# One fused attention and feed-forward kernel, its instruction order replaced by another searched one

## The chip, the cores and the metric

The kernel runs on one core of one Trainium2 chip. The metric is the device time of one execution in microseconds (us), lower is better.

## What is computed

The reference is a linear attention with a complex decay, and a gated feed-forward layer on its output. Batch 4, 8 heads, 768 positions, 48 columns to a head, so 384 columns together; 1024 hidden columns.

```python
mag = np.sqrt(a_re * a_re + a_im * a_im)
scale = np.minimum(mag, 0.999) / (mag + 1e-06)
for t in range(S):                       # per batch and head, S_re and S_im 48 x 48
    new_re = ar * S_re - ai * S_im
    new_im = ar * S_im + ai * S_re
    S_re, S_im = (new_re + kv, new_im)   # kv = outer(k_t, v_t)
    y[:, :, t] = np.einsum('bhd,bhde->bhe', q[:, :, t], S_re)
# x = y with heads side by side; x_prev = x one position earlier
xk = mu_k * x + (1.0 - mu_k) * x_prev
xr = mu_r * x + (1.0 - mu_r) * x_prev
k = np.maximum(xk @ w_k, 0.0)
v = k * k @ w_v
r = 1.0 / (1.0 + np.exp(-(xr @ w_r)))
return r * v
```

## The kernel before, in words

The 4 x 768 positions are cut into 8 units of 384: units 0 and 1 are the two halves of batch 0, and so on. Each unit goes through three phases.

- **gate** (phase `g`): loads the decay, k and q of the unit (`in_gat`, L720, tile `g`) and v (`in_vt`, L727), turns the decay into running logarithms (scans, L797) and phases (scans, L821) on ScalarE (ACT) and VectorE (DVE), and multiplies k and q with them (L811, and L864 as the last step). ACT needs four function tables for it and for the sigmoid; a change of table is the operation L321.
- **attend** (phase `a`): copies parts of `g` to the stacked tile `q` by DMA (L895), transposes keys on TensorE (PE) (L1021, L957), makes the sums of keys and values (L1060 in unit 0, L990 later), adds them up into states on DVE (L1073, L1000), makes scores (L1107, L1102), masks them on DVE (L1123, tile `pt`), and multiplies states and scores with queries and values (L1148). The result is copied from PSUM (L1183) to the tile `xt`; that of head pair 3 goes to `ys` and from there by six small DMAs (L1199) into `xt`. Unit 0 does this pair by pair, the others by two teams of pairs.
- **mix** (phase `m`): the shifted mixes of x (unit 0: L443 on ACT and L447 on DVE; others: L431, L458, a rounded first half L467 or L469 and the rest L472), the first product (L498 in unit 0, L502 later, where each operand is split in two halves and three products are made), relu on ACT (L545), square (L550 on DVE or L552 on ACT), the halves of h (L557 on DVE or ACT, L561 on DVE), the second product (L591), the sigmoid gate (`zr`) and the output (L618, stored by L623).

The weights come in ten pieces (phase `f`, L658, tile `raw`), are put together (phase `w`: L672 and L678, tile `wx`) and are split for units 1 to 7 (phase `s`: L697, L700). 75 fillers of two matmuls each on zeros (phase `x`, L1237) fill PE while unit 0's gate runs.

Nothing schedules at run time or by rules. Each phase records its operations in a `Plan`, and the table `ORDER` gives each operation a place, by phase and unit; `run` sorts by the places and emits, so that the five engines and the DMA queue of SyncE (SP) get their instructions in this order and work them off in it. A data or buffer dependence becomes a wait of the instruction. Two more tables belong to the order: `ON_DVE` names the operations, out of those that both engines can do, that DVE does (the rest is ACT's), and `HOMES` says which buffer of a pool each use takes.

```python
order = [next(places[phase]) if places else i for i, (_, _, phase) in enumerate(self.ops)]
self.queue = sorted(range(len(order)), key=order.__getitem__)
```

Table loads are not in the order: one is emitted ahead of an operation whose function the loaded table lacks.

Of the kernel before, what the change touches and what calls it, by code (L numbers as in the profile page):

```python
# [48 lines left out]
    ("g", 0): (0, 2, 1, 3, 4, 8, 10, 70, 5, 6, 22, 30, 36, 37, 43, 44, 59, 61, 63, 47, 75, 80, 84, 89, 88, 60, 78,  # L49
        79, 85, 92, 87, 81, 82, 83, 101, 103, 108, 90, 91, 111, 110, 137, 93, 94, 100, 102, 143, 109, 121, 114, 117,  # L50
        140, 99, 105, 134, 106, 125, 126, 97, 98, 133, 107, 130, 135, 95, 96, 119, 104, 115, 116, 131, 139, 141, 144,
        142, 136, 145, 161, 138, 156, 157, 172,),
    ("g", 1): (7, 15, 25, 235, 237, 234, 309, 320, 310, 162, 163, 164, 174, 194, 201, 211, 213, 222, 230, 227, 236,
        344, 267, 265, 278, 292, 277, 276, 314, 322, 325, 348, 326, 335, 336, 341, 345, 342, 361, 343, 364, 349, 360,),
    ("g", 2): (287, 295, 288, 472, 474, 112, 354, 357, 367, 384, 393, 400, 413, 414, 415, 425, 427, 424, 444, 445,
        446, 448, 455, 458, 467, 464, 531, 469, 477, 485, 486, 496, 490, 509,),
    ("g", 3): (451, 449, 450, 470, 656, 721, 557, 565, 568, 576, 593, 594, 613, 618, 621, 634, 625, 628, 718, 641,
        645, 650, 622, 644, 640, 633, 659, 669, 671, 688, 693, 700, 698, 714,),
    ("g", 4): (624, 681, 680, 880, 853, 951, 737, 756, 758, 772, 773, 779, 796, 797, 805, 808, 811, 816, 851, 817,
        821, 843, 815, 826, 832, 844, 863, 845, 847, 850, 860, 868, 861, 877,),  # L60
    ("g", 5): (820, 813, 812, 684, 1100, 1032, 893, 894, 916, 922, 935, 957, 960, 966, 968, 974, 970, 969, 1018,
        994, 985, 996, 1003, 1016, 1006, 1004, 1019, 1022, 1023, 1031, 1041, 1046, 1045, 1048,),
    ("g", 6): (999, 998, 1000, 1248, 1238, 1085, 1049, 1053, 1058, 1079, 1097, 1098, 1152, 1162, 1161, 1165, 1179,
        1163, 1181, 1193, 1194, 1195, 1103, 1189, 1167, 1182, 1205, 1202, 1203, 1218, 1219, 1228, 1229, 1233,),
    ("g", 7): (1220, 1188, 1186, 1300, 1487, 1399, 1268, 1272, 1289, 1308, 1329, 1330, 1334, 1338, 1343, 1344, 1356,
        1345, 1614, 1364, 1368, 1406, 1372, 1402, 1407, 1403, 1455, 1409, 1413, 1414, 1422, 1429, 1425, 1432,),
    ("f", 0): (12,),
    ("f", 1): (9,),
    ("f", 2): (50,),
    ("f", 3): (19,),  # L70
    ("f", 4): (67,),
    ("f", 5): (40,),
    ("f", 6): (56,),
    ("f", 7): (32,),
    ("f", 8): (311,),
    ("f", 9): (323,),
    ("w", 0): (71, 182,),
    ("w", 1): (54, 188,),
    ("w", 2): (199, 259,),
    ("w", 3): (200, 260,),  # L80
    ("w", 4): (263, 328,),
    ("w", 5): (299, 338,),
    ("w", 6): (329, 379,),
    ("w", 7): (380, 383,),
    ("w", 8): (421, 431,),
    ("w", 9): (456, 460,),
    ("a", 0): (122, 179, 149, 191, 146, 165, 166, 167, 168, 170, 184, 196, 203, 205, 208, 216, 221, 246, 154, 160,
        158, 239, 243, 242, 229, 212, 219, 197, 169, 173, 171, 186, 187, 190, 193, 204, 209, 210, 215, 217, 226, 177,
        181, 178, 261, 279, 266, 273, 238, 248, 240, 189, 206, 202, 218, 224, 220, 284, 290, 291, 293, 297, 301, 358,
        151, 176, 192, 185, 195, 175, 256, 257, 255, 225, 241, 244, 245, 247, 251, 254, 275, 249, 253, 250, 258, 264,  # L90
        269, 270, 271, 281, 280, 285, 283, 286, 300, 294, 306, 307, 316, 315, 308, 272, 282, 317, 377,),
    ("a", 1): (363, 402, 386, 397, 419, 430, 436, 365, 368, 417, 389, 401, 388, 371, 405, 426, 428, 390, 362, 382,
        391, 394, 392, 369, 370, 381, 395, 396, 399, 406, 411, 412, 374, 378, 376, 398, 409, 404, 418, 423, 429, 432,
        441, 433, 420, 440, 422, 442, 443, 452, 453, 457, 479, 447, 462, 459, 463, 475, 471, 481, 476, 487, 488, 480,
        492, 483, 505, 489, 493, 506,),
    ("a", 2): (543, 537, 519, 567, 559, 517, 513, 518, 595, 504, 578, 574, 515, 544, 514, 590, 554, 510, 586, 570,
        545, 558, 546, 541, 549, 551, 534, 535, 539, 555, 556, 587, 560, 566, 561, 577, 580, 579, 599, 601, 602, 538,
        552, 553, 536, 547, 542, 609, 610, 611, 630, 629, 637, 631, 623, 632, 635, 648, 653, 651, 674, 654, 661, 655,
        663, 658, 676, 678, 662, 664, 679, 803,),
    ("a", 3): (790, 744, 723, 750, 708, 763, 754, 774, 780, 703, 704, 716, 782, 709, 727, 751, 715, 733, 752, 722,  # L100
        728, 748, 735, 747, 757, 762, 734, 740, 749, 764, 765, 766, 741, 767, 742, 745, 770, 771, 776, 777, 783, 781,
        787, 786, 785, 788, 793, 804, 806, 825, 822, 835, 829, 807, 823, 824, 830, 838, 841, 839, 831, 856, 846, 870,
        849, 848, 872, 857, 871, 873,),
    ("a", 4): (874, 881, 911, 914, 952, 948, 937, 879, 913, 941, 926, 864, 865, 890, 950, 927, 882, 910, 891, 895,
        938, 939, 963, 896, 904, 899, 900, 919, 920, 928, 929, 930, 905, 924, 931, 942, 971, 947, 978, 981, 982, 945,
        946, 972, 949, 967, 979, 980, 983, 995, 984, 1002, 1005, 1012, 992, 1011, 1010, 1020, 1026, 1027, 1025, 1021,
        1034, 1050, 1029, 1073, 1067, 1033, 1051, 1074, 1068, 1089,),
    ("a", 5): (1059, 1109, 1125, 1054, 1099, 1128, 1083, 1087, 1093, 1047, 1092, 1084, 1094, 1124, 1066, 1055, 1127,
        1060, 1101, 1121, 1069, 1090, 1080, 1081, 1108, 1130, 1075, 1077, 1076, 1131, 1144, 1145, 1122, 1135, 1132,
        1117, 1139, 1138, 1140, 1148, 1151, 1153, 1168, 1154, 1146, 1170, 1171, 1173, 1174, 1175, 1176, 1177, 1183,  # L110
        1184, 1187, 1185, 1192, 1204, 1196, 1212, 1214, 1236, 1216, 1207, 1208, 1290, 1215, 1237, 1209, 1291,),
    ("a", 6): (1234, 1232, 1262, 1282, 1309, 1269, 1284, 1315, 1270, 1301, 1252, 1253, 1235, 1292, 1274, 1283, 1251,
        1302, 1275, 1239, 1303, 1320, 1335, 1266, 1271, 1267, 1258, 1259, 1294, 1295, 1306, 1307, 1263, 1264, 1265,
        1313, 1322, 1314, 1350, 1352, 1353, 1310, 1346, 1312, 1316, 1321, 1318, 1357, 1358, 1359, 1369, 1375, 1385,
        1386, 1354, 1379, 1378, 1380, 1387, 1382, 1383, 1384, 1392, 1393, 1390, 1388, 1389, 1397, 1394, 1391, 1398,
        1533,),
    ("a", 7): (1427, 1459, 1444, 1433, 1437, 1491, 1443, 1451, 1426, 1485, 1481, 1501, 1445, 1464, 1435, 1486, 1434,
        1458, 1497, 1460, 1488, 1510, 1517, 1449, 1470, 1466, 1456, 1477, 1480, 1482, 1483, 1493, 1494, 1496, 1504,
        1492, 1513, 1505, 1518, 1523, 1524, 1498, 1520, 1521, 1452, 1484, 1467, 1522, 1525, 1537, 1526, 1540, 1543,
        1519, 1529, 1530, 1534, 1542, 1535, 1554, 1539, 1571, 1544, 1546, 1545, 1555, 1556, 1572, 1547, 1557,),  # L120
    ("m", 0): (302, 304, 303, 372, 305, 319, 333, 407, 318, 332, 337, 434, 330, 331, 334, 339, 340, 312, 321, 346,
        347, 359, 366, 324, 327, 350, 356, 373, 385, 313, 351, 352, 375, 410, 403, 353, 355, 387, 408, 416, 435, 491,
        499, 501, 502, 503, 454, 437, 438, 439, 465, 466, 520, 497, 498, 500, 512, 524, 581, 582, 516, 530, 511, 522,
        507, 508, 588, 589, 605, 608, 583, 585,),
    ("m", 1): (494, 523, 532, 533, 521, 527, 528, 540, 584, 603, 604, 548, 562, 563, 550, 572, 575, 686, 564, 569,
        571, 710, 711, 705, 729, 701, 712, 591, 592, 598, 600, 612, 596, 597, 606, 607, 617, 636, 616, 638, 639, 660,
        668, 646, 614, 619, 649, 652, 670, 685, 657, 672, 673, 692, 697, 689, 677, 683, 702, 707, 713, 717, 665, 675,
# [29 lines left out]
        1686, 1688, 1687, 1697, 1693, 1689, 1699, 1700, 1694, 1696, 1692, 1695,),  # L157
    ("s", 0): (461, 468,),
    ("s", 1): (473, 478,),
    ("s", 2): (482, 484,),  # L160
    ("s", 3): (495, 525,),
    ("s", 4): (526, 529,),
    ("s", 5): (573, 615,),
# [1234 lines left out]
```

## Time and profile before

| what | value |
|---|---|
| median of 3 runs (from, to) | 399.31 us (397.34, 399.97) |
| the profiled execution, by the same clock as the runs | 399.91 us |
| its span in the trace | 398.1 us |
| PE busy | 381.8 us (96%), 5855 matmul passes |
| DVE busy | 336.0 us (84%) |
| ACT busy | 291.0 us (73%) |
| granted clock of PE over the span | 0.997 |

The page gives the busy time of each engine over the whole span; a list by stretches shows how that differs along the way, and the rows below take it from there. A wait in the trace is idle time of an engine ahead of an instruction, with what ended it; "issue" stands where the profile shows nothing that it waited for. Matmul ends are modelled, so short waits of PE can lie inside its busy time.

### The profile page before, as it was taken

How to read it: one execution, taken by the hardware profiler on the slowest of the kernel's cores; microseconds unless marked ns; L12 is line 12 of the kernel's file. 1: busy time of each engine (PE TensorE's matmuls, PEld its weight loads, DVE VectorE, ACT ScalarE, POOL GpSimd, SP SyncE). 2: the span in 40 equal slices, each digit the busy share in tenths (PEclk: the TensorE clock that was granted, in tenths of full speed). 3: DMA queues.
4: the chain of work that ended last, by engine and by line, in shares of the span. 5: the costliest groups of instructions: out<-in, count | busy, mean ns of one | idle time of the engine just before them, and what ended most of it. 6: DMA issues, size and time to landing. Idle time of an engine off the chain costs nothing. (4 is left out here: it accounts for less than half of the span.)

```text
span 398.1 us, 13663 instructions
## 1 busy us (share of the span) xinstructions
PE 381.8 (96%) x5855; PEld 349.4 (88%) x5855; DVE 336.0 (84%) x542; ACT 291.0 (73%) x556; POOL 23.8 (6%) x36
## 2 busy tenths in 40 slices
PE   6988889999999999899999999999999999999995
PEld 6977756675899999799989999999999999999994
DVE  6999999999999999899999978988999754555532
ACT  7997889989999996999668875778676721262420
POOL 5203100000000330000000100000000000000000
PEclk9999999999999999999999999999999999999998
DMA  8995466472431544714262331464011420100101
GB/s 272 419 400 103 155 251 219 101 273 62 121 101 63 181 114 130 261 40 122 66 250 86 96 97 56 155 207 107 4 67 31 109 66 4 66 9 2 61 2 64
DMA packets 23138, 49.70 MB, mean 125 GB/s; under 512 B 4864, under 2 KB 16640, under 8 KB 23072
## 3 DMA queue, kind: packets, MB, share of 16 engines
q1 hardware_dynamic: 23072, 48.78, 37.9%
q8 instruction: 47, 0.77, 0.8%
q14 instruction: 19, 0.16, 0.1%
HBM read 31.06 MB, written 4.72 MB: 90 GB/s over the span
## 5 line engine op out<-in xcount | busy, mean ns | idle before, releaser
L502 PE MATMUL bank<-x,w 128*128 128x384 f32 x693 | 127.6, 337 | 0.9 <-ACT xt L1183 0.9
L502 PEld LDWEIGHTS bank<-x,w 128*128 128x128 f32 x693 | 120.1, 188 | 2.2 <-ACT xt L1183 1.0
L591 PE MATMUL o<-hx,w 128*128 128x384 f32 x504 | 94.9, 337 | 0.0
L591 PEld LDWEIGHTS o<-hx,w 128*128 128x128 f32 x504 | 87.3, 188 | 0.2
L545 ACT ACTIVATE r<-bank 128x384 f32<-128x384 f32 x64 | 30.8, 488 | 41.6 <-PE bank L502 34.9
L864 DVE TENSOR_TENSOR g<-g,r 128x768 f32<-128x768 f32 (+1 forms) x24 | 41.7, 1754 | 0.5
L321 ACT ACT_TABLE_LOAD x29 | 37.2, 1283 | 1.3 <-PEq L1387 0.8
L561 DVE TENSOR_TENSOR hx<-h,hx 128x384 fp32r<-128x384 f32 x56 | 30.8, 554 | 5.6 <-ACT hx L557 4.9
L333 ACT ACTIVATE sq<-m 128x1152 f32<-128x1152 f32 (+1 forms) x30 | 28.3, 968 | 7.2 <-DVE m L797 5.0
L1237 PE MATMUL room<-idle 128*128 128x384 f32 (+4 forms) x150 | 29.8, 354 | 3.2 <-POOL idle L392 3.2
L1237 PEld LDWEIGHTS room<-idle 128*128 128x128 f32 x150 | 26.8, 198 | 4.2 <-POOL idle L392 3.2
L472 DVE TENSOR_TENSOR x<-xm,x 128x384 fp32r<-128x384 f32 x42 | 23.1, 552 | 6.3 <-ACT x L469 6.1
L552 ACT ACTIVATE h<-r 128x384 f32<-128x384 f32 x47 | 24.7, 526 | 4.8 <-DMA out_t<-y 2.7
L1148 PEld LDWEIGHTS bank<-q,state 112*48 112x48 f32 x704 | 21.4, 123 | 6.7 <-issue 4.2
L1148 PE MATMUL bank<-q,state 112*48 112x64 f32 x704 | 24.1, 221 | 3.3 <-DVE state L1073 1.4
L1107 PE MATMUL bank<-g 48*64 48x64 f32 x1200 | 25.0, 223 | 2.2 <-DVE g L864 1.1
L1107 PEld LDWEIGHTS bank<-g 48*64 48x64 f32 x1200 | 22.4, 133 | 4.7 <-issue 2.2
L458 DVE SCALAR_TENSOR_TENSOR xm<-dx,mu_sb,xt 128x384 f32<-128x384 f32 x42 | 25.4, 614 | 0.7
L1000 DVE TENSOR_TENSOR state<-bank,state 112x384 f32<-112x384 f32 x35 | 19.4, 554 | 7.5 <-ACT kt L971 3.3
L1209 POOL COPY last<-xt 128x3 f32<-128x3 f32 x4 | 9.9, 2468 | 247.8 <-DMA xt<-ys 164.1
L469 ACT ACTIVATE x<-xm 128x384 fp32r<-128x384 f32 x34 | 17.8, 524 | 6.8 <-DVE xm L458 5.8
L557 ACT CAST hx<-h 128x384 fp32r<-128x384 f32 x34 | 17.5, 514 | 7.1 <-PE o L591 4.2
(97 smaller groups left out, 581.1 us busy)
## 6 DMA issues: line engine op xcount, KB each, us to landing
g<-in_gat SPq DMA_DIRECT2D x18, 768.0 KB, 6.0
raw<-in_w_all SPq DMA_DIRECT2D x9, 767.8 KB, 13.7
v<-in_vt SPq DMA_DIRECT2D x24, 192.0 KB, 3.8
out_t<-y SPq DMA_DIRECT2D x24, 192.0 KB, 2.0
g<-in_gat SPq DMA_DIRECT2D x11, 384.0 KB, 4.6
q<-g SPq DMA_DIRECT2D x84, 48.0 KB, 2.3
q<-g SPq DMA_DIRECT2D x28, 144.0 KB, 2.9
q<-g SPq DMA_DIRECT2D x40, 72.0 KB, 2.2
```

The lines of the kernel that those rows point to most:

```text
L321: nc.scalar.add_instruction(mybir.InstLoadActFuncSet(name=nc.get_next_instruction_name(), act_func_set_id=n, engine=mybir.EngineType.Activ ...
L333: nc.scalar.activation(out=out, in_=in_, func=func, **kw)
L458: nc.vector.scalar_tensor_tensor(out=xm[which, ct], in0=d[ct], scalar=mu_sb[:, which, ct:ct + 1], in1=X[u][:, ct, 0:U], op0=ALU.mult, op1= ...
L502: nc.tensor.matmul(z, lhsT=wt[s[0]][:, part, s[1]], rhs=r[which][:, ct], start=n == 0, stop=n == 3 * NT - 1)
L545: nc.scalar.activation(out=t["r", j], in_=t["f", j], func=AF.Relu, scale=1.0 / W_SCALE)
L552: nc.scalar.activation(out=t["h", j], in_=t["r", j], func=AF.Square)
L561: plain[0].tensor_tensor(out=t["lo", j], in0=t["h", j], in1=t["hi", j].bitcast(F32), op=ALU.subtract)
L591: nc.tensor.matmul(tiles["o", mt][:, cols], lhsT=w, rhs=r[:, cols], start=j == 0 and n == 0, stop=j == NJ - 1 and n == len(parts) - 1 and ...
L864: nc.vector.tensor_tensor(out=g[:, d, 2 * i:2 * i + 2], in0=g[:, d, 2:4], in1=t["r"][:, 1 - i, d].unsqueeze(2).to_broadcast([P, k, 2, U]), ...
L1107: nc.tensor.matmul(y, lhsT=g[:, 2 * i, q], rhs=g[:, 2 * i + 1, q], start=i == 0, stop=i == 1)
L1148: nc.tensor.matmul(t["y", team][s][rows, h // 2 - team[0], c], lhsT=lhsT[:, cols], rhs=rhs, start=(s, h % 2) not in begun, stop=stop)
L1237: nc.tensor.matmul(room[0][:, :n], lhsT=idle[:, :P], rhs=idle[:, :n], start=True, stop=True)
```

## The change

The tables `ORDER`, `ON_DVE` and `HOMES` are replaced; every operation, its operands and its sizes stay. The new tables come from a search over three replays, two of them with late transfers, late refills and longer elementwise work. One line more in `ON_DVE` moves line numbers behind it up by one (L1183 is L1184 after).

```diff
@@ ORDER: all lists; three of them, cut @@
-    ("g", 0): (0, 2, 1, 3, 4, 8, 10, 70, 5, 6, 22, 30, 36, 37, 43, 44, 59, 61, 63, 47, 75, 80, 84, 89, 88, 60, 78,
...
@@ ON_DVE @@
     "abs": (
-        (0, 0), (0, 1), (1, 0), (3, 0), (4, 0), (5, 0), (6, 0), (7, 0),
+        (0, 2), (1, 0), (3, 0), (4, 0), (5, 0), (6, 0),
     ),
     "hi": (
-        (1, 4), (1, 7), (2, 0), (2, 2), (2, 3), (2, 4), (2, 6), (3, 2), (3, 3), (3, 4), (3, 6), (4, 3), (5, 4),
-        (5, 6), (5, 7), (6, 2), (6, 6), (6, 7), (7, 0), (7, 4), (7, 6), (7, 7),
+        (1, 3), (1, 5), (1, 6), (2, 2), (2, 7), (3, 2), (3, 4), (3, 5), (3, 6), (4, 1), (4, 2), (4, 3), (4, 4),
+        (4, 6), (5, 0), (5, 1), (5, 2), (5, 3), (5, 4), (5, 6), (6, 4), (7, 0), (7, 1), (7, 2), (7, 3), (7, 4),
+        (7, 6), (7, 7),
     ),
     "n": (
-        (0, 1), (4, 0), (5, 0),
+        (4, 0), (6, 0),
     ),
     "sq": (
-        (0, 0), (0, 1), (3, 4), (3, 5), (3, 6), (4, 2), (4, 3), (4, 5), (5, 1), (5, 6), (6, 1), (6, 2), (6, 4),
-        (6, 6), (7, 1), (7, 4), (7, 5),
+        (0, 2), (3, 4), (3, 5), (3, 7), (4, 2), (4, 5), (4, 6), (5, 0), (5, 6), (6, 4), (6, 5), (7, 3), (7, 4),
+        (7, 7),
     ),
     "xr": (
-        (1, 2), (2, 0), (2, 1), (3, 0), (5, 1), (6, 1), (7, 0), (7, 1),
+        (1, 2), (2, 1), (3, 0), (3, 1), (4, 0), (5, 2), (6, 0), (6, 1), (7, 0), (7, 1),
     ),
     "y": (
-        (0, 1, 1, 0), (0, 3, 0, 0), (1, 2, 0, 0), (1, 2, 1, 0), (4, 3, 1, 0), (5, 0, 1, 0), (5, 3, 0, 0), (5, 3,
-        1, 0), (5, 2, 0, 0), (5, 2, 1, 0), (6, 0, 0, 0), (6, 0, 1, 0), (7, 0, 1, 0), (7, 3, 0, 0),
+        (1, 2, 1, 0), (3, 2, 1, 0), (4, 3, 1, 0), (4, 2, 1, 0), (5, 2, 1, 0), (6, 3, 0, 0), (7, 0, 0, 0), (7, 3,
+        1, 0), (7, 2, 1, 0),
     ),
@@ HOMES: all but "g"; one of them @@
-    "kt": "010011110011101100010001",
+    "kt": "010000010010010100010101",
```

In `ON_DVE` a key's first number is the unit. "sq" is the square, "hi" the rounded first half of h, "xr" that of a mix, "y" the copy out of PSUM, "n" and "abs" two steps of the phase.

Three places show what that does to the engines. The first is ACT at the end of unit 0's attention, where the results of pairs 1 and 3 are copied out of PSUM (`xt`, `ys`) and the first mix begins (`x`, L443); before, and after it the same place now:

```order
L333 ACTIVATE sq<-m 128x3x384 x2
L1183 COPY ys<-bank 112x3x64
L321 ACT_TABLE_LOAD
L333 ACTIVATE ph<-ph 128x1152
L1183 COPY xt<-bank 112x3x64
L1075 COPY state_109<-bank 112x96
L672 CAST hx<-raw 128x768
L443 ACTIVATE x,stat<-xt,mu_118 128x384
```

```order
L334 ACTIVATE sq<-m 128x3x384 x2
L1184 COPY xt<-bank 112x3x64 x2
L1184 COPY ys<-bank 112x3x64 x2
L322 ACT_TABLE_LOAD
L334 ACTIVATE ph<-ph 128x1152
L1076 COPY state_109<-bank 112x96
L673 CAST hx<-raw 128x768
L444 ACTIVATE x,stat<-xt,mu_118 128x384 x2
```

Both copies of `ys` stand on ACT now, ahead of the table load, where one stood there and one on DVE. The second place is DVE at the same time, from two weight conversions (`wx`) to the first step of the mix (`x`, L447); before, and now:

```order
L678 SCALAR_TENSOR_TENSOR wx<-raw,hx 128x768 x2
L1183 COPY ys<-bank 112x3x64
L1183 COPY xt<-bank 112x3x64
L1073 TENSOR_TENSOR state_108<-bank,state_113 112x96
L811 TENSOR_TENSOR g<-g,sq 128x768 x2
L1073 TENSOR_TENSOR state_110<-bank,state_109 112x96
L811 TENSOR_TENSOR g<-g,sq 128x768
L1073 TENSOR_TENSOR state_111<-bank,state_110 112x96
L1123 TENSOR_TENSOR pt<-bank,mask 128x192
L1073 TENSOR_TENSOR state_112<-bank,state_111 112x96
L1123 TENSOR_TENSOR pt<-bank,mask 128x192
```

```order
L679 SCALAR_TENSOR_TENSOR wx<-raw,hx 128x768 x2
L812 TENSOR_TENSOR g<-g,sq 128x768 x3
L1074 TENSOR_TENSOR state_110<-bank,state_109 112x96
L1124 TENSOR_TENSOR pt<-bank,mask 128x192
L1074 TENSOR_TENSOR state_111<-bank,state_110 112x96
L1124 TENSOR_TENSOR pt<-bank,mask 128x192
L1074 TENSOR_TENSOR state_112<-bank,state_111 112x96
L1074 TENSOR_TENSOR state_113<-bank,state_112 112x96
L1074 TENSOR_TENSOR state_108<-bank,state_113 112x96
L448 SCALAR_TENSOR_TENSOR x<-xt,mu_sb,x 128x384
```

The two copies out of PSUM, `ys` and `xt`, are gone from DVE, and three products (L811) stand together. The third place is SP's queue at the end of unit 0's weight loads, with the first transfers from `g` to the stacked queries (`q01`, `q23`); before, and now:

```order
L658 DMA raw_267<-in_w_all 128x3071
L727 DMA v_273<-in_vt 128x384
L1244 DMA mu_sb_105<-in_mu 128x6
L727 DMA v_324<-in_vt 128x384
L895 DMA q01_114<-g_149 48x384 x2
```

```order
L659 DMA raw_300<-in_w_all 128x3071
L896 DMA q01_114<-g_151 48x384
L728 DMA v_365<-in_vt 128x384
L1245 DMA mu_sb_105<-in_mu 128x6
L896 DMA q01_114<-g_151 48x384
L728 DMA v_438<-in_vt 128x384
L728 DMA v_442<-in_vt 128x384
```

Before, two `v` loads of unit 0 stood among the first seven transfers (not shown) and two more here (one of them of unit 1), ahead of the first `q01`; now the first three `v` loads stand behind it. Further on in the same queue the last `q23` transfer of unit 0 stood between the second and third of the six `xt<-ys` transfers, and stands now ahead of all six.

## Rows read from the trace of the kernel before

**Rows 1.** Stretches: length, busy us (instructions) of PE, PEld, DVE, ACT, POOL; clock, DMA.

```profile
25.00:52.30 27.30, 22.27 (x615) 18.67 (x614) 26.17 (x51) 22.72 (x43) 5.00 (x3) 1.00 0.56 164
...
62.00:165.00 103.00, 101.86 (x1867) 85.28 (x1867) 100.31 (x151) 94.22 (x166) 7.48 (x1) 1.00 0.44 136
...
165.00:265.00 100.00, 98.25 (x1561) 94.45 (x1555) 92.77 (x138) 77.96 (x145) 1.05 (x1) 1.00 0.39 122
...
265.00:393.40 128.40, 127.97 (x1679) 124.44 (x1679) 86.21 (x156) 65.39 (x144) 0.50 (x1) 1.00 0.17 48
```

**Rows 2.** Waits of PE over the span: us in total, times, longest.

```profile
PE bank L1148 <- DVE state L1073: 1.4, 1, 1.4
...
PE bank L1148 <- DMA q<-g: 1.2, 1, 1.2
...
PE bank L1148 <- issue: 1.1, 2, 0.7
...
PE bank L1107 <- issue: 1.1, 2, 0.9
...
PE bank L502 <- ACT xt L1183: 0.9, 1, 0.9
...
PE bank L957 <- ACT zr L333: 0.8, 2, 0.5
```

**Rows 3.** Timeline of PE, 32 to 62 us: start, us, instruction, idle before.

```profile
32.42 1.46 PE L1060 MATMUL bank<-v,kt 64*48 64x48 f32 x96
...
45.02 0.55 PE L1148 MATMUL bank<-pt,v 64*48 64x64 f32 x24
...
51.04 0.85 PE L1148 MATMUL bank<-q,state 112*48 112x64 f32 x20 [1.15 <-DMA q<-g]
...
52.31 9.40 PE L498 MATMUL bank<-x,wx 128*128 128x384 f32 x28
```

**Rows 4.** Timeline of DVE, 23 to 52 us.

```profile
23.66 0.95 DVE L864 TENSOR_TENSOR g<-g,r 128x768 f32<-128x768 f32 x1
...
46.21 0.35 DVE L1183 COPY ys<-bank 112x192 f32<-112x192 f32 x1
...
51.59 0.62 DVE L447 SCALAR_TENSOR_TENSOR x<-xt,mu_sb,x 128x384 f32<-128x384 f32 x1 [0.81 <-ACT x L443]
```

**Rows 5.** Timeline of ACT, 47 to 51 us.

```profile
47.98 1.07 ACT L672 CAST hx<-raw 128x768 f16<-128x768 bf16 x1
50.85 0.61 ACT L443 ACTIVATE x<-xt,mu 128x384 f32<-128x384 f32 x1 [1.80 <-DMA xt<-ys]
```

**Rows 6.** Timeline of SP's DMA queue, 46 to 52 us.

```profile
46.62 1.15 SPq L1199 DMA_DIRECT2D xt<-ys  x2
...
48.45 3.51 SPq L1199 DMA_DIRECT2D xt<-ys  x4
```

**Rows 7.** Groups by line and shape, DVE then ACT: count, busy us, mean ns, idle.

```profile
L550 DVE TENSOR_TENSOR h<-r 128x384 f32<-128x384 f32 x17 | 9.4, 552 | 4.7 <-ACT r L545 4.1 <-ACT h L552 0.5
...
L557 DVE CAST hx<-h 128x384 fp32r<-128x384 f32 x22 | 7.8, 356 | 7.6 <-PE o L591 7.1 <-ACT h L552 0.4
...
L321 ACT ACT_TABLE_LOAD x29 | 37.2, 1283 | 1.3 <-PEq L1387 0.8
...
L552 ACT ACTIVATE h<-r 128x384 f32<-128x384 f32 x47 | 24.7, 526 | 4.8 <-DMA out_t<-y 2.7 <-DVE h L550 0.7 <-DVE hx L561 0.6
...
L557 ACT CAST hx<-h 128x384 fp32r<-128x384 f32 x34 | 17.5, 514 | 7.1 <-PE o L591 4.2 <-DVE h L550 2.6
```

**Rows 8.** Timeline of ACT around a table load.

```profile
12.05 1.28 ACT L321 ACT_TABLE_LOAD   x1
13.35 0.94 ACT L333 ACTIVATE ph<-ph 128x384 f32<-128x384 f32 x2
```

**Rows 9.** The first four v loads (L727), then all xt<-ys: us to landing.

```profile
DMA to landing us min/median/max: 5.2/8.8/12.5
...
xt<-ys SPq DMA_DIRECT2D x48, 24.0 KB, 1.9
```

More of the change, by code (lines that the diff above doesn't have):

```diff
@@ L227 @@
     "g": "01010101",
-    "hx": "0110100101100101011001101010101011100100100010110110100101",
-    "kt": "010011110011101100010001",
+    "hx": "0110010110000110100110010101010101010100101100101001011001",
+    "kt": "010000010010010100010101",
     "ps": (
-        "122001010311343141443410023002240324424303013114244110132001301343241024120040331412320143203113"
-        "133441133130422420324100124104320021014303032424322310032342342431024010323324040241234201400013"
-        "102430432343031321414304231003123240240204113203443233113024334"
+        "041012303232341043114203431001142434404133012211343120130231310124331003240404111204202411423030"
+        "024132420131240113001434321320322404230110034041414321314302002211430200131221244321314041201421"
+        "302313012143431214334144020343022314213040403402141434044103242"
     ),
-    "pt": "01010110100110010110101001100101",
+    "pt": "01001010100101101001010110011010",
     "r": (
-        "010321013003010211232033123132110311103223033101020130203013102320210231013001122121101212130230"
-        "22101233031101202101031302212321202133012100312013002102"
-    ),
-    "v": "201021123013103230201310",
-    "x": "021102022021211011120122100012200200100012210122100102200012011",
+        "021001302001120331021301201212330210320112121002230310033122101031003200322023302302210301202301"
+        "31032212132201022303210130012321033211230103121300120210"
+    ),
+    "v": "210013201301203210301031",
+    "x": "012021211122122011102102022012120021211210100011200102120120200",
 }
```

249 rows, old and new, of the table ORDER are left out of this document.

## The prediction

> **What bounds the kernel now.** I read the stretches first [rows 1]: TensorE (PE) is busy 381.8 of 398.1 us, and the 16.3 us in which it is not lie in four places: 5.03 us in the head from 25 to 52.3 us, 3.3 us in all the rest of its work (1.14 from 62 to 165, 1.75 from 165 to 265, 0.43 later), 4.7 us behind the last matmul at 393.4 (the last `y` product, its store, the end of the program), and what is left, 3.2 us, before the first filler matmul. The last two are the same in both programs: the same memset comes first, and the same gate and value matmuls come last. So an order can win at most 5.03 + 3.3 = 8.4 us, and it can lose any amount.
>
> Whom PE waits for is in the waits [rows 2]: in the head DVE's state sums (1.4), a `q` transfer (1.2) and 0.9 of "issue", which no order removes for certain; behind the head 1.1 and 0.2 of issue, and ScalarE (ACT) for 0.9 on an `xt` copy and 0.8 on sigmoids. Behind these small waits stand two nearly full engines: from 62 to 165 us VectorE (DVE) is idle 2.7 of 103 us and ACT 8.8 [rows 1]. From 265 us on DVE is idle 42 and ACT 63 of 128 us, and PE 0.43: there the order has little to win, and much cover.
>
> The head ends where the first mix matmul (L498) starts, at 52.31 [rows 3]. It starts as soon as the first L447 is done (51.59 + 0.62), L447 waited 0.81 for ACT's L443, and L443 waited 1.80, until 50.85, for `xt<-ys` transfers [rows 4, 5]. Two of those were issued at 46.62, behind DVE's copy of `ys` at 46.21; four more came from 48.45 on [rows 4, 6], with a `q` transfer between them.
>
> **The change, part by part.** *Work moved between DVE and ACT.* From the table of what DVE does, with the means of [rows 7]: squares on DVE 17 to 14 and copies out of PSUM of 384 columns 4 to 1, together 6 x 0.55 off DVE (the copies taken at L550's time) and 6 x 0.526 onto ACT; first halves of h 22 to 28, 6 x 0.356 onto DVE and 6 x 0.514 off ACT; first halves of xr 8 to 10, 2 of the same size the same way. What is left, two copies of 192 columns and four phase steps of which one has 1152 columns, I put at 2.1 us off DVE and 2.8 onto ACT, an estimate by columns from the same rows. Sum: DVE -3.3 + 2.1 + 0.7 - 2.1 = -2.6 us. ACT +3.2 - 3.1 - 1.0 + 2.8 = +1.9, and four more table loads (29 to 33 run, counted in the two orders), 4 x 1.283 = 5.1: +7.0 us. All four stand behind the 25th L545 of 64, in the second half of the work, where ACT is idle 22 of 100 us and then 63 of 128 [rows 1]. I take them at nothing; their cover is the queue of ready mix matmuls, and without it each costs 1.28.
>
> A rule of the Trainium skill speaks against this part. In the trace ACT's next operation starts 1.30 us after the load ahead of it began (12.05 to 13.35) [rows 8]: no drain is seen. The page "ScalarE: Activation LUTs", section "What ACT_TABLE_LOAD costs", gives the load as 1283 ns and a drain of about 1380 ns with it, 2.66 us for a switch; by that the four would be 10.6 us instead of 5.1, an estimate from the page. The load's length agrees with the row; the drain does not show in it.
>
> *The end of the head.* Ahead of the first L447, DVE loses two PSUM copies of 192 columns and two phase steps of 384, about 1.3 us by columns; ACT gets the same ahead of the first L443, about 1.6. PE now does the values of pair 1 first and those of pair 3, which make `ys`, second; the second of the two ends at 45.57 [rows 3]. Both `ys` copies follow on ACT, behind two xt copies of that size. At some 0.3 us each (half of L552, estimated) the last can end near 46.3 [rows 7], and SP issues four `xt` transfers in a row, with all `q` transfers ahead of them. At 0.58 us for an issue and 1.9 to land [rows 6, 9], block 0 is there at 46.3 + 1.2 + 1.9 = 49.4. ACT came to L443 at 49.05 (47.98 + 1.07) [rows 5] and has 1.6 more, 50.7, less what it takes back of its earlier waits. L443 so starts between 49.4 and 50.7 instead of 50.85, a gain of 0.15 to 1.45. I take 0.9, as the `q` transfer for which PE waited at 51.04 also goes earlier.
>
> The loss at this place: SP now holds the three value loads of unit 0 behind a `q` transfer that waits for the first L864, which ends at 24.6 [rows 4]. With the issues between, the third `v` is issued near 27. Of the four early `v` loads (192 KB each) before, one landed 12.5 us later and none in under 5.2, behind the weights [rows 9]. The same weights are in the queue now, issued long before, and 0.8 MB of `v` ahead of them is not, so I put the landing at about 31, some 4 us behind the issue. The sums that need it (L1060) started at 32.42 [rows 3]. If the landing took the 5.2 us and half a us more, PE would wait, and a late sum moves the whole head: bounds of this place -1.45 and +1.5.
>
> *From 62 to 265 us.* DVE's work ahead of comparable steps is less: 0.9 us ahead of the last L864 of unit 2, 3.5 ahead of that of unit 3, 4.4 ahead of the last L561 of mix 1, where some of it only goes behind (instructions counted in both orders, with means as in [rows 7]). ACT's is more: 1.6 us ahead of the 8th L545, 1.4 ahead of the 16th, 2.9 ahead of the 24th. DVE had 2.7 us of idle to give and gets more; ACT had 8.8 and gives up 1.4 to 2.9 [rows 1]. The two shifts are of one size and opposite signs, in chains that go back and forth between the two engines, so I set them against each other and take 0.4 us off the 1.7 of waits on ACT [rows 2]; bounds: all 1.7 gone, or 2.9 more.
>
> *Sum.* 399.91 (the profiled execution) - 0.9 - 0.4 = 398.6. That execution stands 0.6 above the median of the three runs, 399.31, so 398.0.
>
> **The rivals.**
> A, PE waits no more: everything but issue goes, 5.03 - 0.9 in the head, 1.7 behind it and 0.4 at the end, 6.2 us: 393.1. For: DVE, the fuller engine, has less ahead of nearly every step. Against: ACT has more, and it was ACT for which PE waited behind 62 us. Chance 0.20.
> B, ACT sets the pace: the 2.9 us ahead of the 24th L545 come onto the path, and one of the new loads ahead of an L545 that frees a PSUM bank, 1.28: 399.3 + 4.2 = 403.5; with all four loads 407.3. It decides once ACT's idle time from 62 to 165 us falls below some 3 us, for then nothing of its delay is taken back. For: ACT is 91% busy there. Against: 8.8 us are left [rows 1]. Chance 0.19. By the page of above the loads alone would be 10.6 and the time 399.3 + 2.9 + 10.6 = 412.8, an estimate that the row does not bear out.
> C, nothing to see: the matmuls are the same and PE is 98% to 99.7% busy behind 62 us, so waits move and their sum stays: 399.3; with the late `v` of above, 400.8. Chance 0.26.
> My forecast, about one us less, 397 to 399: 0.35.
>
> **How the numbers follow.** 1% is 4.0 us, about what a measurement of this kernel tells from no change (the three runs lie 2.6 us apart). Below 395.3 only A ends, above 403.3 only B: faster 0.20, within 1% 0.61, slower 0.19. The range may leave out 2 in 10: it takes in A down to 393.5 and B up to 403.5.
>
> **What would show it.** Right: L498 starts at 51.0 to 52.0; no wait of PE for a `q` transfer; ACT's idle time from 62 to 165 us at 5 to 8 us and DVE's above 3; 33 loads of 1.28, none with a wait of PE behind it. Wrong: L1060 waits for `v` near 31 us (C or worse); PE's idle time from 62 to 265 us goes above 5 us, with ACT's relus and copies as releasers (B); or the 5.03 of the head fall below 2 (A).

## The result, and the profile after

The changed kernel takes 395.51 us (median of 20 runs) against 399.44 for the kernel before, a ratio of 0.9907 with a 95% interval of 0.9883 to 0.9931. In each kernel one of the 20 took over 2,000 us; the ratios here and below leave out executions over 1.5% above the fastest of their kernel. The direction and the range of the prediction hold. Its size does not: 1.3 us were forecast, 3.9 came.

| | before | after |
|---|---|---|
| profiled execution | 399.91 us | 395.26 us |
| its span | 398.1 | 393.5 |
| first mix matmul starts (L498; L499 after) | 52.31 | 51.03 |
| from there to the end of the last matmul | 341.02 | 337.66 |
| busy: PE, DVE, ACT | 381.8, 336.0, 291.0 | 380.7, 330.1, 296.9 |
| table loads | 29 | 33 |

Of the 4.64 us between the two profiled executions up to the last matmul, 1.28 lie ahead of the first mix matmul and 3.36 behind it. The line numbers of after are one higher than those of before.

The stretches of the changed kernel, in the columns of [rows 1] (PE, PEld, DVE, ACT, POOL, clock, DMA):

```profile
25.00:52.30 27.30, 23.78 (x619) 19.11 (x618) 24.99 (x53) 24.46 (x51) 4.51 (x3) 1.00 0.62 168
62.00:165.00 103.00, 102.91 (x1930) 87.52 (x1929) 100.35 (x145) 97.00 (x175) 0.19 (x1) 1.00 0.47 140
165.00:265.00 100.00, 99.53 (x1519) 96.24 (x1518) 92.79 (x144) 85.25 (x154) 0.88 (x1) 1.00 0.43 129
```

PE's idle time falls from 5.03 to 3.52 us in the head, from 1.14 to 0.09 from 62 to 165 us and from 1.75 to 0.47 from 165 to 265. What PE still waits for (over the span; us in total, times, longest):

```profile
PE bank L1108 <- issue: 1.4, 2, 0.9
PE bank L1022 <- DVE stat L805: 0.5, 1, 0.5
PE bank L1108 <- DVE g L865: 0.5, 1, 0.5
PE bank L1149 <- DVE pt L1124: 0.5, 1, 0.5
PE bank L991 <- ACT r L546: 0.5, 1, 0.5
```

Beside [rows 2]: the 1.4 for a state sum (one of 0.3 is left), the 1.2 for a `q` transfer, the 0.9 for ACT's `xt` copy and the 0.8 for ACT's sigmoids are gone.

The end of the head, from four timelines (ACT, then SP's queue, DVE and PE; start, us, instruction, idle before), to be set beside [rows 3 to 6]:

```profile
44.98 0.54 ACT L1184 COPY ys<-bank 112x192 f32<-112x192 f32 x2 [0.64 <-PE bank L1149]
45.54 1.28 ACT L322 ACT_TABLE_LOAD   x1
46.83 1.16 ACT L334 ACTIVATE ph<-ph 128x1152 f32<-128x1152 f32 x1
...
48.96 0.61 ACT L444 ACTIVATE x<-xt,mu 128x384 f32<-128x384 f32 x1
```

```profile
45.55 2.43 SPq L1200 DMA_DIRECT2D xt<-ys  x4
```

```profile
47.89 0.96 DVE L812 TENSOR_TENSOR g<-g,sq 128x768 f32<-128x768 f32 x1 [0.47 <-DMA g<-in_gat]
...
50.24 0.61 DVE L448 SCALAR_TENSOR_TENSOR x<-xt,mu_sb,x 128x384 f32<-128x384 f32 x1
```

```profile
51.03 2.23 PE L499 MATMUL bank<-x,wx 128*128 128x384 f32 x6
```

Both `ys` copies run on ACT from 44.98 to 45.52, four of their transfers are issued in a row from 45.55, and the first L444 starts at 48.96 without a wait. It ends at 49.57, yet the first L448 comes only at 50.24: now DVE is last, with an L812 that waited 0.47 for a load and the state sums behind it.

Behind the head the reading that matters is what ended ACT's idle time. The waits of ACT from 62 to 165 us, before:

```profile
ACT r L545 <- DMA out_t<-y: 2.2, 1, 2.2
ACT r L545 <- PE bank L502: 1.5, 2, 1.2
ACT sq L333 <- DVE m L797: 0.8, 1, 0.8
ACT w L697 <- DVE wx L678: 0.8, 1, 0.8
ACT w L697 <- DVE w L700: 0.7, 2, 0.4
```

and after:

```profile
ACT kt L972 <- PE bank L991: 1.3, 1, 1.3
ACT w L698 <- DVE w L701: 1.1, 2, 0.6
ACT hx L558 <- PE o L592: 0.7, 1, 0.7
ACT ys L1184 <- PE bank L1149: 0.4, 1, 0.4
ACT kt L967 <- PE bank L958: 0.4, 1, 0.4
```

With the smaller rows counted in, ACT waited 3.8 us for DVE, 2.2 for a transfer and 1.7 for PE; now it is 1.8, nothing and 3.0. One reading: where ACT waits for PE, PE has work at hand; where ACT waits for DVE or for a store, PE's next operand may stand behind it. By this reading ACT's idle time fell from 8.8 to 6.0 us, and more of what is left is harmless. That is a reading of two profiles. The experiments price ACT's lateness; none of them tests whom ACT waits for.

### The profile page after: what moved, and what is told of

It reads as the page before. It is cut to its first block, busy times and chain, and to the rows that moved or that the text cites. A ratio compares the mean times of both kernels' runs of the same rounds, so it can differ in the third digit from the quotient of the medians.

```text
span 393.5 us, 13648 instructions
## 1 busy us (share of the span) xinstructions
PE 380.7 (97%) x5855; PEld 349.3 (89%) x5855; DVE 330.1 (84%) x539; ACT 296.9 (75%) x563; POOL 16.0 (4%) x36
## 4 chain that ended last, share of the span: by engine, by line
PE 87%; ACT 6%; DVE 3%; DMA 2%; issue 1%; SPq 0%; DVEq 0%; ACTq 0%
PE bank L503 30%; PE o L592 26%; PE bank L1149 9%; PE bank L499 6%; PE bank L1108 5%; PE bank L991 4%; PE bank L958 4%; ACT sq L334 2%; PE bank L1103 2%; DMA g<-in_gat 1%; PE room L1238 1%; ACT L322 1%; DVE g L865 1%; DMA out_t<-y 1%; ACT sq L777 1%
## 5 line engine op out<-in xcount | busy, mean ns | idle before, releaser
L553 ACT ACTIVATE h<-r 128x384 f32<-128x384 f32 x50 | 26.2, 523 | 11.0 <-DVE h L551 4.3
L1238 PE MATMUL room<-idle 128*128 128x384 f32 (+4 forms) x150 | 30.6, 358 | 3.2 <-POOL idle L393 3.2
L558 ACT CAST hx<-h 128x384 fp32r<-128x384 f32 x28 | 14.4, 516 | 15.4 <-PE o L592 15.2
L499 PE MATMUL bank<-x,wx 128*128 128x384 f32 x66 | 22.5, 490 | 0.0
L812 DVE TENSOR_TENSOR g<-g,sq 128x768 f32<-128x768 f32 (+1 forms) x12 | 21.6, 1814 | 0.5 <-DMA g<-in_gat 0.5
```

The source lines that it names most:

```text
L499: nc.tensor.matmul(z, lhsT=wx[s[0]][:, s[1]], rhs=hi[which][:, ct], start=ct == 0, stop=ct == NT - 1)
L553: nc.scalar.activation(out=t["h", j], in_=t["r", j], func=AF.Square)
L1238: nc.tensor.matmul(room[0][:, :n], lhsT=idle[:, :P], rhs=idle[:, :n], start=True, stop=True)
```

## Experiments

In the runs below line numbers differ with the printed length of the tables: L498 of before is L390 in the three runs with spliced orders, L405 in the two with an exchanged engine table, L431 and L434 in the two with the moved L812, L501 or L502 in those with added work. Ratios are to executions of the kernel before that ran along with each (medians 399.28 to 400.19). "From L498" is the time from the start of the first mix matmul to the end of the last matmul in the profiled execution.

| run | median us | ratio (95%) | L498 starts | from L498 |
|---|---|---|---|---|
| before | 399.44 | 1 | 52.31 | 341.02 |
| after | 395.51 | 0.9907 (0.9883 to 0.9931) | 51.03 | 337.66 |
| first 475 steps new | 403.33 | 1.0117 (1.0059 to 1.0174) | 50.88 | 346.13 |
| first 475 steps old | 397.01 | 0.9951 (0.9918 to 0.9984) | 52.77 | 337.01 |
| first 740 steps new | 398.09 | 0.9965 (0.9937 to 0.9994) | 53.83 | 339.95 |
| after, L812 moved | 395.65 | 0.9893 (0.9854 to 0.9933) | 50.41 | 337.04 |
| before, engine table of after | 420.93 | 1.0531 (1.0484 to 1.0579) | 57.27 | 356.05 |
| after, engine table of before | 405.76 | 1.0154 (1.0106 to 1.0202) | 51.80 | 346.45 |
| before, ACT + 3.85 us | 402.71 | 1.0059 (1.0041 to 1.0078) | 53.40 | 343.61 |
| after, ACT + 3.85 us | 396.67 | 0.9913 (0.9884 to 0.9942) | 50.84 | 339.15 |
| before, DVE + 4.41 us | 404.00 | 1.0109 (1.0074 to 1.0144) | 53.15 | 344.79 |
| after, DVE + 4.41 us | 398.57 | 0.9972 (0.9948 to 0.9995) | 50.90 | 340.88 |
| after, four more table loads | 397.49 | 0.9975 (0.9941 to 1.0010) | 51.37 | 339.53 |
| after, L812 moved, two fillers | 395.22 | 0.9886 (0.9856 to 0.9916) | 50.86 | 336.73 |

### Where along the way: spliced orders

Three kernels take a first part of the steps in one order and the rest in the other. Of the table `ORDER`, the beginning of phase mix 7 as an example (cut; in the first run the late phases keep the order of before):

```diff
@@ ORDER, against the changed kernel @@
-    ("m", 7): (1596, 1664, 1666, 1667, 1602, 1616, 1618, 1576, 1593, 1606, 1607, 1582, 1594, 1598,
+    ('m', 7): (1588, 1650, 1659, 1660, 1589, 1594, 1602, 1577, 1580, 1598, 1599, 1578, 1579, 1582,
```

> The first 475 of the 1701 recorded steps stand in the new order (about the first 85 us: the whole head and the start of unit 1's attention), all others in the order of before; the engine table goes with each part, and 2 buffer homes differ. Theory R (each stretch's own order made its own gain): the first mix matmul starts at about 51.0 instead of 52.3 as in the changed kernel, the time behind it stays that of before, so 0.9 to 1.6 us less than before, some 398. Rival H (the head's lead is what frees PE later: engines that come out of the head further ahead make fewer waits for the rest of the run): most of the 3.7 us appears, 396 or less. Rival N (an order only works as a whole; at the seam the engines wait): no gain or a loss, 399.4 or more.

Measured: 403.33 us, slower than either kernel. The head is as in the changed kernel (50.88). The loss lies behind the seam, in a PE wait and a DVE wait (timelines), the six `xt<-ys` transfers ahead of them (us to landing) and a lower clock (a stretch):

```profile
101.74 2.61 PE L849 MATMUL bank<-ident,g 128*128 128x128 f32 x11 [4.10 <-ACT zr L225]
```

```profile
97.11 0.56 DVE L323 TENSOR_TENSOR dx<-xt 128x384 f32<-128x384 f32 x1 [4.43 <-DMA xt<-ys]
```

```profile
DMA to landing us min/median/max: 1.9/3.4/6.5
```

```profile
102.00:104.00 2.00, 2.00 (x11) 2.00 (x11) 1.97 (x6) 1.19 (x5) 0.00 (x0) 0.50 0.40 96
```

The `ys` copies themselves are early (ACT, 87.19; before, 87.65 and 88.58). But at the seam SP issues five loads of `v` and `g` from 87.19 to 89.90, right ahead of the `xt<-ys` transfers, and one of the first two of these lands 6.5 us after its issue, where none of the six took over 3.0 in the kernel before. DVE's first step of mix 1 waits 4.43 us for it, ACT behind DVE, and PE stands 4.10. From 102 us on the granted clock is 0.50, the lower level (1.2 GHz), and by 108 it is back. This is rival N: the run tells nothing between R and H.

> The mirror of the run above: the first 475 steps in the order of before (to about 85 us), the rest in the new order; 6 buffer homes differ. Theory R: the first mix matmul at 52.3 as before, and the stretch behind it 2.3 to 3.4 us shorter, so 396 to 397. Rival H: no lead out of the head, so no gain behind it: 398.8 to 399.6. Rival N: 399.4 or more, with PE waiting near 85 us.

Measured: 397.01 us. The first mix matmul starts at 52.77, later than in the kernel before, and from there the run takes 337.01 us, no more than the changed kernel's 337.66. Its stretches behind the head:

```profile
62.00:165.00 103.00, 102.76 (x1869) 86.73 (x1869) 99.96 (x148) 95.91 (x170) 0.19 (x1) 1.00 0.43 129
165.00:265.00 100.00, 99.68 (x1582) 96.24 (x1577) 93.51 (x141) 85.98 (x155) 0.23 (x1) 1.00 0.42 130
```

So the gain behind the head needs nothing from the new head. R holds for this side, H falls.

> The first 740 steps in the new order (to about 160 us), the rest in that of before. Theory R: the gain of the head and the 1.05 us of PE's waits between 62 and 165 us, and none of the 1.3 us of waits from 165 to 265: 2.0 to 2.8 us less than before, 396.6 to 397.4. Rival H: all of the 3.7 us, 395.7. Rival N: 399 or more.

Measured: 398.09 us, 0.7 more than R's upper end. Two things stand out in its profile, and both tell little of the order. The first is the clock in the head (PE's timeline, then stretches):

```profile
26.38 0.55 PE L913 MATMUL bank<-ident,g 128*128 128x128 f32 x3 [1.01 <-DVE stat L696]
...
28.38 1.67 PE L999 MATMUL bank<-g 48*64 48x64 f32 x46 [0.48 <-DVE g L756]
```

```profile
28.00:30.00 2.00, 1.62 (x47) 1.51 (x47) 1.72 (x4) 1.96 (x3) 0.00 (x0) 0.57 0.26 78
30.00:32.00 2.00, 2.00 (x8) 1.86 (x8) 1.98 (x3) 0.91 (x3) 0.00 (x0) 0.50 0.71 206
```

The head's order is that of the changed kernel, where the same two waits were shorter and the clock was 1.00:

```profile
25.55 0.55 PE L1022 MATMUL bank<-ident,g 128*128 128x128 f32 x3 [0.52 <-DVE stat L805]
...
27.54 1.02 PE L1108 MATMUL bank<-g 48*64 48x64 f32 x46 [0.49 <-DVE g L865]
```

In the spliced kernel it stood at 0.50 from 30 to 34 us, and the first mix matmul came 2.8 us later. That belongs to this execution: only 3 of this run's 12 had a mean clock under 0.997, so it does not explain the median. The second is the seam, a wait of 1.72 us for a state sum at 152.9. From 62 to 150 us PE idles only 0.16 us, about as in the changed kernel (0.09).

### Order or engine table

The table `ON_DVE` alone is exchanged; its lines on squares, in the run on the order of before:

```diff
@@ ON_DVE, against the kernel before @@
-        (0, 0), (0, 1), (3, 4), (3, 5), (3, 6), (4, 2), (4, 3), (4, 5), (5, 1), (5, 6), (6, 1), (6, 2), (6, 4),
-        (6, 6), (7, 1), (7, 4), (7, 5),
+        (0, 2), (3, 4), (3, 5), (3, 7), (4, 2), (4, 5), (4, 6), (5, 0), (5, 6), (6, 4), (6, 5), (7, 3), (7, 4),
+        (7, 7),
```

> The order of before with the new table ON_DVE alone (which engine does the squares, first halves, copies); 29 table loads as before. Theory O (the order makes the gain; the table by itself only shifts about 2 us from DVE to ACT): within 0.5 us of before plus what the old order pays for steps it did not place, 399 to 401. Rival E (the relief of DVE, 6 us of busy time, makes the gain behind the head): 396 to 397.5, with PE's waits from 62 to 265 us under 1.2 us instead of 2.9.

> The new order with the old table ON_DVE: the mirror of the run above; 33 table loads as in the changed kernel. Theory O: most of the gain stays, 395.5 to 397.5. Rival E: the gain behind the head is gone, 398 to 399.5. The head alone is expected to lose some of its 1.3 us here, since one ys copy and some phase steps are back on DVE ahead of the first mix step.

Measured: 420.93 and 405.76 us. Both theories fall. The same relief of DVE that stands in the faster kernel costs the old order 5.3%, and the old table costs the new order 10 us. One place of the first run shows how. PE's scores of the last pair, and ACT ahead of them:

```profile
51.39 1.67 PE L1014 MATMUL bank<-g 48*64 48x64 f32 x48 [2.77 <-ACT xt L1090]
```

```profile
45.66 0.32 ACT L1090 COPY ys<-bank 112x192 f32<-112x192 f32 x1 [2.04 <-PE bank L1055]
46.00 1.17 ACT L240 ACTIVATE sq<-m 128x1152 f32<-128x1152 f32 x1
...
51.03 0.30 ACT L1090 COPY xt<-bank 112x192 f32<-112x192 f32 x1
```

The same copy in the kernel before:

```profile
47.19 0.30 ACT L1183 COPY xt<-bank 112x192 f32<-112x192 f32 x1
```

The copy of `ys` that was DVE's at 46.21 [rows 4] is now ACT's, at its old place in the order, ahead of two `sq` steps. ACT works in order, so it stands 2.04 us until PE has made that bank, and what is behind it, up to the next copy, comes 3.8 us later than before (1.4 of it stood ahead of this wait, as ACT was free at 43.61 instead of 42.19). Behind PE's wait the granted clock was 0.50 from 52 to 56 us. The new order has its `ys` copies behind those steps. The head loses 5.0 us. Another 15.0 lie behind it and were not taken apart: PE's idle time rises from 1.14 to 2.83 us from 62 to 165 and from 1.75 to 4.74 from 165 to 265.

### Which engine sets the pace

Work that changes nothing is added at three places: table loads on ACT, or two subtractions and a copy on a tile of its own on DVE (6 x 0.556 + 3 x 0.36 = 4.41 us by the trace).

```diff
+EXTRA = (500, 600, 700,)
...
             done.add(i)
+            if self.at in EXTRA:
+                self.extra()
...
+            plan[0].extra = lambda: load_table(loaded[0])
             plan[0].run(ORDER)
```

> The kernel before with three more table loads on ACT (3 x 1.28 = 3.85 us, work that changes nothing in the result), at the steps 500, 600 and 700 of 1701 (about 94 to 142 us), where ACT has 8.8 us of idle time from 62 to 165. If ACT paces that stretch (what the prediction's rival B rests on), the end moves by most of it, +2.5 to +3.9: 402 to 403. If DVE paces it, ACT's idle time takes it: +0 to +1, 399.4 to 400.4.

> The changed kernel with the same three loads at the same steps (about 92 to 140 us); ACT has 6.0 us of idle time there. If the new order has used up ACT's room, +2.5 to +3.9: 398 to 399.4. If work further ahead still covers it: +0 to +1, 395.5 to 396.5. Set beside the same addition to the kernel before, it tells whether the new order is more or less exposed to a late ACT.

> The kernel before with three times two subtractions and a copy of 128x384 on DVE (a tile of its own; nothing in the result changes; about 4.4 us by the means of L550 and L557 in rows 7), at the same three steps (about 94 to 142 us) at which ACT got 3.85 us more. DVE has 2.7 us of idle from 62 to 165. Theory D (DVE is the tighter of the two engines there): +3.3 to +4.4, more for each us than ACT's addition cost the same kernel (+2.5). Rival: the lead DVE has over PE takes it, +0 to +2.

> The changed kernel with the same DVE work at the same steps; DVE's idle there is 2.65 us, as before, but DVE has 3.5 us less ahead of the gate of unit 3. Theory D with the new order giving DVE more lead: +1 to +2.5, clearly less than in the kernel before. Rival: DVE is as tight as before: +3.3 to +4.4, 399 to 400.

Measured, from L498 in the profiled executions: before, ACT's 3.85 us cost 2.59 (0.67 for each us) and DVE's 4.41 cost 3.77 (0.85). After, ACT's cost 1.49 (0.39) and DVE's 3.22 (0.73). Each is one execution less another: three that differ by one moved step and two fillers (337.66, 337.04, 336.73) lie 0.9 us apart. By the ratios the additions cost +2.4 and +4.4 us before, +0.2 and +2.6 after, each known to 1 or 2 us. So in the old order both engines lay on the path, which goes back and forth between them. In the new one ACT has gained room by both measures, though it is 5.9 us busier. DVE's price is still the larger. Whether it fell as well is open: hardly in the profiles (0.85 to 0.73), as much as ACT's in the ratios (by 1.8 us against 2.2). For DVE after, neither expectation is met: 3.22 lies a little below the rival's, 2.6 a little above theory D's.

How the two engines hang together is seen in PE's waits from 85 to 165 us with the work added on DVE, before:

```profile
PE bank L960 <- ACT zr L336: 2.2, 1, 2.2
PE bank L1110 <- DVE g L867: 0.7, 1, 0.7
PE bank L505 <- DVE state L1003: 0.7, 1, 0.7
```

The largest wait names ACT, which got nothing added: ACT's L472 waits 2.18 us for DVE's `xm` (L461), and the sigmoid behind it holds PE's bank, so DVE's delay reaches PE through ACT. The releaser is the last link, not the cause. In the run above that took the first 475 steps in the new order, PE lost its 4.10 us at the same place. DVE there, in the kernel before and in the changed one:

```profile
94.92 0.56 DVE L431 TENSOR_TENSOR dx<-xt 128x384 f32<-128x384 f32 x1 [0.18 <-DMA xt<-ys]
95.40 2.55 DVE L864 TENSOR_TENSOR g<-g,r 128x2304 f32<-128x2304 f32 x1
97.87 1.14 DVE L458 SCALAR_TENSOR_TENSOR xm<-dx,mu_sb,xt 128x384 f32<-128x384 f32 x2
```

```profile
92.51 0.55 DVE L432 TENSOR_TENSOR dx<-xt 128x384 f32<-128x384 f32 x1
93.09 1.15 DVE L459 SCALAR_TENSOR_TENSOR xm<-dx,mu_sb,xt 128x384 f32<-128x384 f32 x2
94.16 2.55 DVE L865 TENSOR_TENSOR g<-g,r 128x2304 f32<-128x2304 f32 x1
```

The old order has a step of 2.55 us between `dx` and the `xm` that ACT needs, the new one has it behind both. With the work added on DVE the changed kernel shows no wait of PE for this sigmoid. So this is one place where ACT got room. In the kernel before PE waited only 0.31 us here, and what the place is worth was not tried alone.

### The price of a table load later on

```diff
+EXTRA = (1000, 1100, 1200, 1300,)
```

> The changed kernel with four more table loads (4 x 1.28 = 5.1 us on ACT, no change in the result) at the steps 1000, 1100, 1200 and 1300 of 1701, in the second half, where the four new loads of the change stand. The prediction took such loads at nothing: +0 to +0.6, 395.5 to 396.1. By the rival (each with PE's wait behind it): up to +5.1, 400.6.

Measured: 397.49 us, 2.0 more than the changed kernel by the medians (2.7 by the ratios) and 1.87 from L498, of 5.13 us of loads: 0.36 for each us. One of the four is seen with a wait of PE behind it (PE's waits from 205 to 300 us, then ACT):

```profile
PE bank L961 <- ACT zr L337: 1.0, 1, 1.0
```

```profile
225.83 1.28 ACT L325 ACT_TABLE_LOAD   x1
227.12 0.87 ACT L337 ACTIVATE zr<-bank 128x384 f32<-128x384 f32 x2
```

ACT is idle 14.75 us from 165 to 265 in the changed kernel, and still a load there is not free: it counts where it stands, here ahead of two sigmoids whose banks PE wants back. Whether the change's own four loads cost anything was not tried. At this price they would be worth up to 1.9.

### Two variants of the changed kernel

```diff
@@ ORDER, against the changed kernel @@
-    ("g", 1): (12, 79, 9, 244, 251, 248, 307, 358, 288, 153, 162, 171, 191, 196,
+    ('g', 1): (12, 79, 9, 244, 251, 248, 307, 358, 287, 153, 162, 171, 191, 196,
```

(The moved step's own place goes from 284 to 301; the steps between move up by one, as seen here.)

> The changed kernel with one step moved: the third product of unit 1 on DVE (L812, 0.96 us, which waited 0.47 for its transfer and stood ahead of the state sums and of the first mix step) goes behind the first L448. If the first mix matmul (51.03) is set by DVE's queue, L448 starts when ACT's L444 ends, at 49.6 instead of 50.24, and the matmul at 50.4; if PE is then fed to the end, the time falls by 0.6, to 394.9. Rival: behind the head the same waits come back elsewhere (the gate of unit 1 is late by 1 us), and the time stays at 395.5 or rises by up to 1.

Measured, DVE and PE:

```profile
49.62 0.61 DVE L380 SCALAR_TENSOR_TENSOR x<-xt,mu_sb,x 128x384 f32<-128x384 f32 x1
```

```profile
50.41 1.56 PE L431 MATMUL bank<-x,wx 128*128 128x384 f32 x4
```

The place is exactly as expected: DVE's queue set the end of the head. The profiled execution keeps the 0.62 and took 394.01 us in all. The median is 395.65, no different from the changed kernel's within the interval.

```diff
+EXTRA = (146, 154,)
...
+            def extra():
+                for _ in range(FILL_N):
+                    nc.tensor.matmul(room[0][:, :U], lhsT=idle[:, :P], rhs=idle[:, :U], start=True, stop=True)
+            plan[0].extra = extra
             plan[0].run(ORDER)
```

> The changed kernel with the third L812 behind the first L448 as in the run before of that name, and two more fillers on PE, where it waited 0.52 and 0.49 us in the changed kernel: ahead of the first key transposes (25.5 us) and between the two first scores (27.5). In one profiled execution of another order with the same head these two waits were 1.01 and 0.48 us, and behind them the granted clock stood at 0.50 from 30 to 34 us; the first mix matmul came at 53.8 instead of 51.0. If these waits bring the lower clock, the fillers keep it away, fewer executions show a mean clock under 0.997, and the median falls by 0.5 to 1 below 395.5. Rival: the clock falls regardless, and the time stays at 395.5, or the fillers delay the scores and it rises by 0.3.

Measured: 395.22 us, the lowest median here, 0.3 below the changed kernel and not told from it by the intervals. PE no longer idles where it did (stretches):

```profile
24.00:26.00 2.00, 2.00 (x13) 1.95 (x12) 2.00 (x6) 1.98 (x5) 0.00 (x0) 1.00 1.02 428
26.00:28.00 2.00, 2.00 (x56) 1.60 (x54) 1.62 (x6) 1.99 (x2) 0.00 (x0) 1.00 0.67 239
```

All six executions had a mean granted clock of 0.998 or more and lie between 394.12 and 395.47 us. Of 19 executions of the changed kernel 8 had less than 0.997, with a median of 397.2 against 395.2 for the others. Were the chance still 8 in 19, six without one would come up in 4 of 100 tries. That speaks for the theory, and six executions don't prove it: the run with the moved L812 and no fillers, the nearer comparison, has only 2 of 6 under 0.997.

## Why the prediction was right, and where its size was off

- **The range.** It is 10 us wide and was drawn to take in most of A and B, so that the time lies in it says little. The forecast's own 397 to 399 was missed by 1.5 us. Of the two terms of its sum one was near, the head, and one far too small, 62 to 265 us.
- **The bounds.** "An order can win at most 5.03 + 3.3 = 8.4 us" is no strict bound. PE's idle time fell by 3.5 us, and 1.1 came out of its busy time (381.8 to 380.7) with the same 5855 passes, whose own lengths add up to 410.1 us in both profiles. The Trainium skill says why, on the page "Perfetto Trace Analysis", section "Tensor Engine Instruction (MATMUL, LD_WEIGHTS)": a matmul's reported end is computed, not observed. The trace agrees: equal lengths with another busy time fit short waits that lie inside it.
- **Work moved.** ACT was put at +7.0 us and its busy time is +5.9; DVE was put at -2.6 and is -5.9. The prediction added up lengths of steps, and busy time counts steps that overlap only once. By lengths ACT has +7.5, and the steps moved off DVE make the -2.6 (three phase steps, not the four that are named). Steps that didn't move took 1.5 us less on DVE, such as nine `wx` steps with 8.6 us instead of 9.4; the last 1.8 us is overlap.
- **Table loads at nothing.** 33 ran, each of 1.283 us, and none shows a wait of PE behind it, as the prediction asked. But the assumption that the second half covers any load is wrong: four more cost 1.9 us from L498, with a PE wait behind one. The Trainium skill, on the page "ScalarE: Activation LUTs", section "What ACT_TABLE_LOAD costs", adds a drain to a switch; no load read here shows it. In the changed kernel ACT's next operation starts 1.29 us after the load at 45.54, and behind each later load, if it waits for no other engine, by 1.30.
- **The head.** -0.9 was taken, -1.28 came, inside the bounds. The reason holds to the transfers and then changes (of PE's waits in the head it had left out 1.1 us for DVE's L864). ACT's first L444 starts at 48.96, earlier than the 49.4 to 50.7 of the prediction, since PE's product ahead of the `ys` copies ends at 44.91 instead of 45.57, the copies start at 44.98 and four transfers go out in a row. DVE, which the prediction didn't count as late there, then sets the end, by 0.6 us, as the moved L812 shows. L499 at 51.03 lies in the forecast 51.0 to 52.0, and PE waits for no `q` transfer.
- **The late `v`.** The landing was put at 31, L1060 at 32.42; L1061 starts at 32.44 with no wait for `v`. The margin is small: in the execution with the moved L812 the same step waited 0.44 us for it.
- **62 to 265 us, the failed step.** "The two shifts are of one size and opposite signs, in chains that go back and forth between the two engines, so I set them against each other and take 0.4 us". PE's idle time there fell by 2.33 us, and from L498 on the run is 3.36 shorter, more than the 1.7 of waits on ACT that were given as the bound of the gain (and 0.5 of these lie behind 265 us). Of the 3.36, 2.04 is PE's idle time and 1.32 its busy time. The runs show what was wrong. With the head of before the rest still takes 337.0 us, so the gain is the rest's own. The work moved decides nothing by itself: the same table, the same shifts from DVE to ACT, makes the new order 10 us faster and the old one 21 us slower. And a us of ACT costs 0.67 in the old order and 0.39 in the new, so the order gave ACT the room that the prediction took as given up. It had judged ACT by its idle time (8.8 down to 6.0, as forecast), and that told nothing of the price. That it matters whom ACT waits for fits the two profiles and was not tested.
- **The signs to look for.** ACT's idle time from 62 to 165 us is 6.0, as forecast. DVE's was to rise above 3 and stays at 2.65. DVE does more of the later work in that stretch, it seems: PE gets through more in it too (1930 matmuls instead of 1867).
- **The rivals.** A's mechanism, PE waits no more, is what happened behind the head, and only partly in it, so the time lies between A's 393.1 and the forecast. Whether its chance of 0.20 was too little one outcome can't tell. B (ACT sets the pace) has its place in the runs, but in the kernel before: there ACT's work cost 0.67.

Which moved steps make the gain behind the head stays open; the one place seen above is not enough. The spliced orders cut it by time, and two of the three lost as much at their seams (a wait of 4.10 us with a lower clock behind it, one of 1.72) as the pieces that were to be told apart. The orders of PE and of SP's queue and the buffer homes changed with the rest, and none of them was exchanged alone, so ACT's room is a part of the cause that the runs show, and perhaps not all of it.

## What to carry to other kernels

Don't price a shift of work between engines by busy or idle time: put a few us of empty work on each engine, and read the price of a us from the end. Take more than one execution for it, since one is known to about 1 us here. Read an engine's idle time by what ended it: here more of it behind the bound engine, and less behind a neighbour or a store, went with a lower price. A searched order and its engine table belong together: here either one with the other's partner was slower than both kernels (405.8 and 420.9 us). And look at the seam when only a part of such an order is taken: one splice of three brought what its part was worth, two lost at the seam.

## What the runs showed of the hardware

In one profile the granted clock fell to the lower level with only short waits of PE close ahead of it: it stood at 0.50 from 30 to 34 us behind waits of 1.01 and 0.48. In the changed kernel waits of 0.52 and 0.49 at the same two places left it at 1.00, and so did 0.91 and 0.48 in the run with the moved L812. Single longer ones left it there too: 1.41 us ahead of 38.44 in the kernel before, and 1.72 ahead of 152.93 in the very run with the fall. So the length of one wait doesn't decide it, and what does stays open. The Trainium skill, on the page "TensorE: Matmul & The Clock Gate", section "Why this matters for your kernels", ties such a fall to a long idle gap of PE. The run with 4.10 us of idle fits that, the one with 1.01 does not. It is nearer to the section "A second HAM failure mode: psum-queue depth-cycling" of that page, which names short idle times that follow each other.
